# Strassen in a mixture of experts: 512 moving columns per weight tile in the first product, a new layout for the expert phase, a halved last tile

## Chip, cores, metric

One core of one Trainium2 chip. The metric is device time in microseconds (us), median of several executions. Traces are of one execution each. Engines in the profile: PE is TensorE, PEld its weight loads, DVE VectorE, ACT ScalarE, POOL GpSimd, SP the queue of the sync engine. A matmul here has a weight tile of 128 x 128, which is loaded first (98 ns), and 256 or 512 moving columns that pass it; its result goes into a bank (`ps`, 128 x 512 in fp32), from which ACT or DVE takes it (an eviction).

## The reference

Linear attention makes x (4608 tokens x 512), a Sinkhorn routing makes a weight P for each token and expert, and eight experts run densely:

```python
for e in range(E):                       # E = 8, D = 512, F = 1024, N = 4608
    h = np.maximum(x @ w1[e], 0.0)       # first product, "up"
    ye = h @ w2[e]                       # second product, "down"
    out += P[:, e:e + 1] * ye
```

## The kernel before

Tokens go in nine groups of 512. Attention and expert 0 (plain matmuls) share the first 250 us. Experts 1 to 7 use Strassen's scheme with seven products in both up and down. The sums of quadrants that it needs are DVE instructions. The kernel writes its work as a list of operations with their inputs and outputs. A scheduler of its own, which has a model of durations, fixes the order on each engine before the program is built.

```python
    def product(bank, lhs, rhs, nk, r, first, takes=(), wk=()):   # one Strassen product
        for i in range(2):
            for k in range(nk):                    # nk = 2 in up, 4 in down
                pe(256, ... matmul(bank()[:, 256*i:256*i+256], lhsT=lhs(k, i), rhs=rhs(k), ...))

    def up7(A, g, X, hT, r0):                      # one group; fp: pair of feature blocks
        # x1: keep, x2: keep, x3: keep + add, x4: relu all accumulate in the same bank x[fp];
        def keep(fp, n):                           # ACT copies a bank to SBUF
            act(512, ... scalar.copy(out=u[fp][n](), in_=x[fp]()))
        def add(bank, fp, n, i, j):                # DVE: relu(bank + kept copy) -> hT
            dve(515, ... ADD_SAT ...)
        # (cut)
    def down8(e, g, hT, w2):                       # the very last group: plain, four tiles
        for ts in (2, 3, 0, 1):
            py = new("P1")
            # eight matmuls of 512 columns, one eviction (DVE, 512 columns), one store of 256 KB

    ORDER = "X1 x10 w10 x11 X2 x20 y10 x21 Z1 y11 X3 w11 x30 x31 x40 x41 w20 Y1 w21 X4 Z2".split()
    for e in range(1, E):
        # (cut) load_w, sums_w
        for g in (range(NG) if e < E - 1 else [8, *range(8)]):
            X = load_x(g)                          # sums of x, kept in DRAM: four per group
            un = up7(A7, g, X, hT, ["up0"])
            for n in ORDER:                        # up of group g, mixed with down of group g-1
                ...
            dn = down7(e, g, hT, B7)               # seven products, four DVE sums of 1024 elements
```

One pass of ORDER is called a step here: 56 up matmuls and 56 down matmuls of 256 columns.

The softmax here doesn't subtract the row's maximum and nothing guards it: scores larger than these inputs give would overflow.

## Time and profile before

| | before |
|---|---|
| time, median of 6 | 1026.59 us (1026.03 to 1026.82) |
| PE idle in the expert phase | 0.0 us; the matmuls set the pace |
| instructions on PE | 9469 recorded matmuls, 9504 loads |

How to read it: PE is the bound; the prediction shows its lines.

### The profile page before, as it was taken

What the parts mean: (1) busy time and instruction counts of PE and PEld (TensorE: products, weight loads), DVE (VectorE), ACT (ScalarE), POOL (GpSimd) and SP (SyncE); (2) the same over time, 40 slices, a digit from 0 to 9 for tenths busy, and PEclk for the clock granted to TensorE, in tenths of its full rate; (3) what the DMA queues carried; (4) which work ended last, traced back from release to release, by engine and by line L of the source; (5) the groups of instructions that cost most, each with busy time, mean ns of one, the idle gap of its engine ahead of it and who ended that gap; (6) DMA issues with size and microseconds to landing.
All of it is one profiled execution on the core that took longest, in us unless ns stands there. A gap on an engine that the chain in (4) does not pass through costs nothing.

```text
span 1026.8 us, 24281 instructions
## 1 busy us (share of the span) xinstructions
PE 1008.1 (98%) x9469; PEld 837.9 (82%) x9504; DVE 823.5 (80%) x1600; ACT 703.9 (69%) x1530; POOL 458.5 (45%) x480
## 2 busy tenths in 40 slices
PE   7899999999999999999999999999999999999998
PEld 4666666645888888888888888888888888888886
DVE  7999989987888887787777877787778877787775
ACT  7999999834888766666666666666665666666663
POOL 5768664400334444444444434544444433444342
PEclk9999999999999999999999999999999999999999
DMA  9999978170232611161115211341116111614333
GB/s 235 192 197 179 177 137 130 37 154 19 85 104 85 124 42 42 47 129 43 48 46 112 54 43 42 75 102 42 42 46 131 42 42 43 130 36 125 133 124 124
DMA packets 112501, 96.03 MB, mean 94 GB/s; under 512 B 54145, under 2 KB 87041, under 8 KB 112385
## 3 DMA queue, kind: packets, MB, share of 16 engines
q1 hardware_dynamic: 80576, 70.55, 26.5%
q0 software_dynamic: 31648, 23.86, 16.6%
q8 instruction: 74, 1.21, 0.5%
q14 instruction: 43, 0.34, 0.1%
q10 hardware_dynamic: 160, 0.07, 0.0%
HBM read 94.98 MB, written 14.16 MB: 106 GB/s over the span
## 4 chain that ended last, share of the span: by engine, by line
PE 93%; ACT 2%; DVE 1%; DMA 1%; SPq 1%; issue 1%; POOL 0%; DVEq 0%; ACTq 0%
PE ps L1273 74%; PE ps L573 17%; PE ps L856 2%; DMA acc<-in_q_dram 1%; ACT q L569 1%; ACT k L569 0%; SPq L495 0%; ACT wx L569 0%; SPq L551 0%; PE ps L885 0%; DMA xd<-S 0%; DVE ps L864 0%; DVE hT L1305 0%; DVE m L565 0%; POOL wx L761 0%
## 5 line engine op out<-in xcount | busy, mean ns | idle before, releaser
L1428 POOL TENSOR_TENSOR acc<-acc,V 128x512 f32<-128x512 f32 x248 | 314.8, 1280 | 484.5 <-ACT V L1425 426.7
L1301 ACT COPY U<-ps 128x512 f32<-128x512 f32 x378 | 217.0, 586 | 166.2 <-PE ps L1273 150.9
L1305 DVE CUSTOM_DVE_ANT_0 hT<-ps,U 128x512 bf16<-128x512 f32 x378 | 254.6, 687 | 87.7 <-PE ps L1273 59.9
L1425 ACT ACTIVATE V<-ps,P 128x256 f32<-128x256 f32 x496 | 208.1, 473 | 90.7 <-PE ps L1273 82.1
L1413 DVE SCALAR_TENSOR_TENSOR acc<-ps,P,acc 128x256 f32<-128x256 f32 x372 | 159.1, 478 | 69.5 <-PE ps L1273 69.2
L1273 PEld LDWEIGHTS <-S 128*128 128x128 bf16 x1984 | 194.1, 98 | 22.6 <-issue 0.2
L1273 PEld LDWEIGHTS <-T 128*128 128x128 bf16 x1512 | 148.0, 98 | 17.2
L1273 PEld LDWEIGHTS <-hT 128*128 128x128 bf16 x1488 | 145.6, 98 | 16.8
L1273 PE MATMUL ps<-X,T 128*128 128x256 bf16 x1008 | 152.4, 273 | 0.0
L1273 PE MATMUL ps<-T,S 128*128 128x256 bf16 x1056 | 135.8, 273 | 0.0
L1273 PEld LDWEIGHTS <-wx 128*128 128x128 bf16 x1152 | 112.7, 98 | 13.6 <-issue 0.2
L1181 DVE TENSOR_TENSOR S<-hT 128x1024 bf16<-128x1024 bf16 x124 | 87.2, 712 | 10.1 <-ACT hT L1310 9.9
L1273 PEld LDWEIGHTS <-w 128*128 128x128 bf16 x864 | 84.5, 98 | 9.8
L1273 PE MATMUL ps<-xT,wx 128*128 128x256 bf16 x576 | 88.4, 273 | 0.1
L1273 PE MATMUL ps<-X,wx 128*128 128x256 bf16 x576 | 86.8, 273 | 0.0
L1310 ACT ACTIVATE hT<-ps 128x512 bf16<-128x512 f32 x126 | 73.2, 606 | 9.8 <-PE ps L1273 9.8
L1273 PE MATMUL ps<-wx,hT 128*128 128x256 bf16 x560 | 77.6, 273 | 0.0
L1273 PE MATMUL ps<-xT,T 128*128 128x256 bf16 x504 | 76.7, 273 | 0.0
L573 PE MATMUL ps<-xT,w 128*128 128x512 bf16 x270 | 70.5, 379 | 0.7
L573 PE MATMUL ps<-w,hT 128*128 128x512 bf16 x276 | 69.8, 379 | 0.7 <-ACT q L569 0.2
L1273 PE MATMUL ps<-T,hT 128*128 128x256 bf16 x496 | 69.2, 273 | 0.0
L1273 PE MATMUL ps<-xT,w 128*128 128x256 bf16 x432 | 66.5, 273 | 0.0
(129 smaller groups left out, 1426.5 us busy)
## 6 DMA issues: line engine op xcount, KB each, us to landing
X<-xd SPq DMA_DIRECT2D x126, 256.0 KB, 2.7
wx<-in_moe_w_dram POOLq DMA_DIRECT2D x8, 1024.0 KB, 12.4
v_m<-in_v_dram SPq DMA_DIRECT2D x15, 512.0 KB, 5.6
out_dram<-acc SPq DMA_DIRECT2D x14, 512.0 KB, 2.9
w<-in_moe_w_dram POOLq DMA_DIRECT2D x6, 1024.0 KB, 12.1
xd<-S SPq DMA_DIRECT2D x18, 256.0 KB, 2.1
qk<-in_k_dram POOLq DMA_DIRECT2D x12, 256.0 KB, 5.5
qk<-in_q_dram POOLq DMA_DIRECT2D x12, 256.0 KB, 6.4
```

The source lines that it names most:

```text
L569: act(el, lambda: nc.scalar.activation(out=dst(), in_=src(), func=ACT.Exp, bias=0.0, scale=scale), r, w)
L573: nc.tensor.matmul(out_, lhsT=lhsT, rhs=rhs, start=start, stop=stop)
L856: pe(65, lambda j=j: nc.tensor.matmul(pn()[:, j * D1:j * D1 + D1], lhsT=s["T"][x]()[:, j % 2, 2 * h + j // 2, :] if j < 4 else r["T"][x]() ...
L1181: lambda: f.tensor_tensor(out=out_(), in0=x(), in1=y(), op=op), r, w, **kw)
L1273: pe(256, lambda i=i, k=k, z=z: nc.tensor.matmul(bank()[:, 256 * i:256 * i + 256], lhsT=lhs(k, i), rhs=rhs(k), start=first and z, stop=k = ...
L1301: act(512, lambda: nc.scalar.copy(out=u[fp][n]().rearrange("p a b -> p (a b)"), in_=x[fp]()), [x[fp]], [u[fp][n]])
L1305: dve(515, lambda: nc.vector._custom_dve(ADD_SAT, out=out_(fp, i, j), in0=bank[fp]().rearrange("p (a b) -> p a b", a=2), in1=u[fp][n](), s ...
L1310: act(512, lambda: nc.scalar.activation(out=out_(fp, i, j), in_=x[fp]().rearrange("p (a b) -> p a b", a=2), func=ACT.Relu, bias=0.0, scale ...
L1413: dve(320, lambda n=n, ts=ts: nc.vector.scalar_tensor_tensor(out=acc[g][:, ts, 256 * j:256 * j + 256], in0=bank()[:, 256 * n:256 * n + 256 ...
L1425: act(370, lambda n=n: nc.scalar.activation(out=u()[:, n, :], in_=bank()[:, 256 * n:256 * n + 256], func=ACT.Copy, bias=0.0, scale=P[:, 4 ...
L1428: pool(695, lambda: nc.gpsimd.tensor_tensor(out=acc[g][:, 2 * i:2 * i + 2, 256 * j:256 * j + 256], in0=acc[g][:, 2 * i:2 * i + 2, 256 * j: ...
```

## The change

Its intent: fewer, wider matmuls in up (two groups share a weight tile), no X sums loaded for the first expert, buffers fitted to that, and a shorter end. The core of the diff:

```diff
+    hx = hp.tile([128, 8192], BF16, name="hx")          # h of expert 0; later TB, S, V lie over it
+    ring(hp, [128, 4, 512], BF16, "h0", 0, 4, hx, [0])
+    ring(hp, [128, 1024], BF16, "TB", 0, 3, hx, half)
-    ring("s_p", [128, 1024], BF16, "T", 9)
-    ring("s_p", [128, 4, 256], BF16, "S", 5)
+    for slot in range(6):                                # h of the pairs, one tile of six slots
+        ring("s_p", [128, 2, 2, 512], BF16, f"H{slot}", 1)
+    ring("s_p", [128, 1024], BF16, "T", 4)
-    for i in fill:
+    for i in fill[:-8]:                                  # expert 0's last eight down tiles ...
         expert0(i)
+    for i in range(4):
+        up0(8, i)
+    def wide(bank, lhs, rhs, r, first, takes=(), wk=()):
+        for k in range(2):
+            pe(512, lambda k=k: nc.tensor.matmul(
+                bank().rearrange("p (a b) -> p a b", a=2), lhsT=lhs(k), rhs=rhs(k), ...))
     # in down7: four sums of 1024 elements become, for each half fp,
+            sub(dve, 512, s(0), h(1, 0), h(1, 1), ALU.add, ...)
+            sub(dve, 512, h(1, 0), h(0, 0), h(1, 0), ALU.subtract, ...)      # in place
+            sub(dve, 512, s(1), s(0), h(0, 0), ALU.subtract, ...)
+            sub(dve, 512, s(2), h(0, 1), s(1), ALU.subtract, ...)
+        def halves_(ts):                                 # the last tile
+            for part in range(2):
+                tile_(ts, 256 * part, 256)
+                store(g, ts, 1, part)                    # 128 KB, on the ACT queue and on SP
+    END = "X1 p2 Y1 X2 Z1 p3 X3 Z2 X4 p0 p1".split()     # down of group 6 mixed with group 7's tiles
+    early, dn = [plain(8)], plain(7)                     # ... mix with the first Strassen steps
+    pairs = [(g, g + 1) for g in range(0, 8, 2)]
```

Group 8 stays single. All lines of the new kernel are shifted: up's wide matmul is L1316, all matmuls of `product` are L1307, the adds L1364, the copies L1360, the sums L1199.

## The prediction

> **What bounds the kernel now.** I read five views, from coarse to fine. First the page: its busy row, and the chain that ended last.
>
> ```profile
> PE 1008.1 (98%) x9469; PEld 837.9 (82%) x9504; DVE 823.5 (80%) x1600; ACT 703.9 (69%) x1530; POOL 458.5 (45%) x480
> ...
> PE 93%; ACT 2%; DVE 1%; DMA 1%; SPq 1%; issue 1%; POOL 0%; DVEq 0%; ACTq 0%
> ...
> L1273 PE MATMUL ps<-X,T 128*128 128x256 bf16 x1008 | 152.4, 273 | 0.0
> L1273 PE MATMUL ps<-T,S 128*128 128x256 bf16 x1056 | 135.8, 273 | 0.0
> ```
>
> TensorE is busy for all but 18.7 us, and the chain runs through it. The last column of the two groups (idle before) is 0.0: in the Strassen phase no matmul waits. But 98% busy says only that matmuls overlap (273 ns each, far fewer ns apart), so next I took the stages, by windows. Columns: length, then PE, weight load, DVE, ACT, POOL.
>
> ```profile
> 205.85:250.51 44.66, 44.43 (x211) 20.32 (x214) 36.11 (x95) 16.28 (x28) 0.77 (x1) 1.00 0.41 89
> 250.51:258.68 8.17, 8.10 (x73) 7.03 (x72) 5.25 (x11) 7.45 (x14) 0.00 (x0) 1.00 0.29 98
> 258.68:1015.20 756.52, 756.52 (x6929) 677.87 (x6929) 590.99 (x1062) 489.65 (x1024) 324.06 (x260) 1.00 0.30 74
> 1015.20:1026.80 11.60, 7.02 (x33) 3.02 (x31) 4.08 (x7) 0.00 (x0) 0.58 (x1) 0.93 0.48 182
> ```
>
> From 258.68 to 1015.20 TensorE is never idle at full clock; DVE is at 78% and ACT at 65%. The idle time before 205 us is in attention, which the change does not touch. What is left to win: the rhythm of the matmuls, about 0.5 us around the start of the phase, and the tail. Third, the rhythm, from the chain in order of time and the timeline:
>
> ```profile
> 258.68 756.68 PE ps L1273 x6928
> ```
>
> ```profile
> 219.31 1.89 PE L573 MATMUL ps<-xT,w 128*128 128x512 bf16 x8
> 221.03 1.89 PE L573 MATMUL ps<-w,hT 128*128 128x512 bf16 x8
> ...
> 241.66 8.51 PEld L573 LDWEIGHTS <-hT 128*128 128x128 bf16 x40
> ...
> 241.88 8.79 PE L573 MATMUL ps<-w,hT 128*128 128x512 bf16 x39
> ...
> 250.51 0.60 PE L1273 MATMUL ps<-xT,wx 128*128 128x256 bf16 x4
> ```
>
> A matmul of 256 columns costs 756.52 / 6928 = 109.2 ns. One of 512 costs (250.51 - 241.88) / 40 = 215.75 ns (40 loads; one matmul record is missing). The eight between 219.31 and 221.03 give 215 ns. I use 215.7. Two of 256 are 218.4, so a merge of two saves 2.7 ns. Lastly the tail, timeline:
>
> ```profile
> 1015.20 7.07 PE L573 MATMUL ps<-wx,hT 128*128 128x512 bf16 x31
> ...
> 1018.33 5.09 SPq L1151 DMA_DIRECT2D out_dram<-acc  x4
> ...
> 1022.31 0.75 DVE L1362 SCALAR_TENSOR_TENSOR acc<-ps,P,acc 128x512 f32<-128x512 f32 x1 [0.91 <-PE ps L573]
> ```
>
> The last matmul ends at 1022.27, its eviction at 1023.06, the span at 1026.8: 4.5 us of eviction, store and end.
>
> [...]Here loads take 98 ns under a matmul of 109 ns and never hold one up; the rhythm decides[...]. [...]In the trace, 1024-element differences start 0.60 us apart and 512-element ones 0.33. [...]The trace has 2.6 us median from issue to landing for a 256 KB store, with its data moved in some 0.7 us.
>
> **The change, part by part.**
>
> *Wide products.* The code's first product (up) is seven Strassen products of 8 matmuls, 56 per group and expert; the second (down) is 56 too. Check: 63 up steps and 62 down steps give 7000 matmuls, the sum of the counts of that line on the page. Of nine groups, eight are paired: 7 experts x 8 groups x 56 = 3136 matmuls of 256 columns become 1568 of 512. Saving: 1568 x 2.7 ns = 4.2 us, all on the path, since TensorE alone sets the time there. The 1568 loads that fall away (98 ns each) were hidden and give nothing. The ninth group and all downs stay at 256. A pair of steps does the same arithmetic: one step goes from 112 x 109.2 = 12.23 us to 28 x 215.7 + 56 x 109.2 = 12.16 us.
>
> *Evictions.* The same count and size: per step six copies on ACT, six adds on DVE, two relus. A PSUM bank now holds two groups of one feature block instead of two feature blocks of one group.
>
> *Down's sums on DVE.* Four of 1024 elements become eight of 512: 8 x 0.33 - 4 x 0.60 = +0.24 us per step of 12.16. By starts, DVE has now about 6 x 0.60 adds + 6 x 0.41 reads + 4 x 0.60 sums + 0.53 weight sums = 9.0 us of 12.2; then 9.2, or 76%. By busy records it goes from 78% to some 82%. Off the path.
>
> *Memory.* Each expert loads three X tiles per pair rather than four; the first loads none, using them where they were made. SP loads drop from 126 x 256 KB to an estimated 81 x 256 KB. Those loads land in 2.7 us behind 12 us steps, so nothing. T shrinks from nine buffers to four: three are in use by one expert, one is spare, so the next expert's second and third weight sums must wait for products in the old expert's last step. The code asks for s2 and s3 before the next first product. Their buffers come free about mid-step, some 5 us early; a sum takes 0.6. I expect no stall.
>
> *The phase's start.* Expert 0's last eight down tiles (8 x 1.73 = 13.8 us) may now mix with the first Strassen steps. Before, those steps had no down work, and 250.51 to 258.68 has 72 matmuls, worth 7.86 us: 0.3 us lost. Routing ends at 242.6, four weight sums at about 245, so the tiles also fill what comes before. Gain 0.2 us.
>
> *The tail.* Work on TensorE is the same (8 x 215.7 against 16 x 109.2 for the last tile, +0.02). The last eviction falls from 0.75 to an estimated 0.44 (the trace's 256-column one), and 128 KB moves in about half of 0.7 us. That is 0.65 us. But group 6's 1 MB of output used to leave from 1015.5, under seven us of matmuls; now its down ends just ahead of the last two tiles, so that 1 MB and the tiles share the DMA engines at 400 GB/s in the last 4 us, which may return half. Gain 0.3 us.
>
> Sum: 4.2 + 0.2 + 0.3 = 4.7 us. I set 0.3 us against it for new short waits where the fixed order no longer fits: 1026.47 - 4.4 = 1022.1.
>
> **The rivals.** (1) *Evictions become the bound.* Two matmuls fill a bank in 0.43 us, one more DVE instruction per two; the order was made from a model of times. For: DVE at 80%, its share of the chain 1%, waits of ACT behind DVE of 14.8 us in the phase. Against: fill time per bank is the same, and TensorE waited 0.0 us before. A wait of 0.1 us in each of 62 steps gives back everything and makes 1028; a wait of 0.05 makes 1025. (2) *Buffers.* A stall at each of six changes of expert, from T or the single-buffered S tiles, at 0.5 to 1 us: 1025 to 1028. For: no spare memory. Against: the time in hand worked out above. (3) *The gain is hidden anyway*: if a strided moving operand (two runs of 256) costs a few ns at the seam, the wide matmul takes 218 and the time is 1026. No row of this trace shows such an operand, neither for nor against. (4) *More than the rhythm*: if loads took time that 109.2 ns hides, halving them would give 1568 x 98 = 154 us, or -15%.[...]
>
> **Range and chances.** The floor is everything working: 4.2 + 0.3 + 0.65 = 5.2 us, 1021.3, less scatter. Runs of before differ by 0.8 us. Upward lie the waits of rivals 1 and 2, which I think partial and unlikely. Range 1020.6 to 1025.0. 2% is 20.5 us; only a breakdown of the order, or rival 4, gets there: faster 0.02, within 0.96, slower 0.02.
>
> **What would show it.** Wide matmuls 215 to 216 ns apart (218 or more proves rival 3); some 5432 matmuls in the phase; TensorE idle still near 0.0 us between experts (else rival 2) and within steps (rival 1); DVE's busy share near 82%; the phase about 4 us shorter; the last eviction 0.44 us, and under 4.5 us from last matmul to end. If the time is below 1020 or above 1026, an amount or a wait that I have not seen is at work.

4.2 + 0.2 + 0.3 = 4.7 us, less 0.3 for waits, 4.4, and 1026.47 - 4.4 = 1022.1. Each term was worked out or estimated from the trace of before. There the DMA engines move 399 to 412 GB/s at their peaks between 990 and 1027 us, and the last 256 KB store moves its data between 1023.9 and 1024.7 us.

## More of the kernel before

DVE is the nearest other engine. Its groups, from the page (instruction, count, busy us, mean ns of one, idle before it and who ended that):

```profile
L1305 DVE CUSTOM_DVE_ANT_0 hT<-ps,U 128x512 bf16<-128x512 f32 x378 | 254.6, 687 | 87.7 <-PE ps L1273 59.9
...
L1181 DVE TENSOR_TENSOR S<-hT 128x1024 bf16<-128x1024 bf16 x124 | 87.2, 712 | 10.1 <-ACT hT L1310 9.9
```

The adds wait for PE, not PE for them. The sums take 685 ns as a rule; the mean of 712 hides a few long ones (up to 947 ns), which come up again under fill_first.

## The result, and the profile after

| | before | after |
|---|---|---|
| time, median of 6 | 1026.59 us | 1022.57 us (1021.99 to 1022.86) |
| ratio | | 0.9961, 95% interval 0.9948 to 0.9974 |

Ratios are the mean time of one kernel's runs over that of the other's of the same rounds, so not quite the ratio of the medians. The class is "same" (within 2%), and the interval lies below 1.

The page of the changed kernel: busy row, chain, and groups.

```profile
PE 1007.1 (99%) x7944; PEld 686.1 (67%) x7944; DVE 853.2 (84%) x1833; ACT 701.6 (69%) x1530; POOL 466.8 (46%) x480
...
PE 95%; ACT 2%; DVE 1%; issue 0%; POOL 0%; DMA 0%; DVEq 0%; ACTq 0%
...
L1364 DVE CUSTOM_DVE_ANT_0 hs<-ps,U 128x512 bf16<-128x512 f32 x378 | 253.0, 687 | 35.7 <-PE ps L1316 15.0
...
L1316 PE MATMUL ps<-X,T 128*128 128x512 bf16 x448 | 129.0, 379 | 0.3 <-ACT U L1360 0.2
...
L1199 DVE TENSOR_TENSOR hx<-hx,hs 128x512 bf16<-128x512 bf16 x124 | 64.2, 518 | 0.0
```

PE has 1560 fewer loads than before and the same bound. DVE rose from 80 to 84% of the span. The idle time ahead of its adds fell from 87.7 to 35.7 us: it still keeps up, with less in hand. By windows (length; PE, PEld, DVE, ACT, POOL busy):

```profile
203.95:258.15 54.20, 54.20 (x264) 24.56 (x261) 41.90 (x101) 27.01 (x48) 0.98 (x2) 1.00 0.32 64
258.15:1013.95 755.80, 755.47 (x5410) 529.02 (x5407) 622.19 (x1302) 484.14 (x1017) 332.36 (x260) 1.00 0.24 59
1013.95:1020.70 6.75, 3.21 (x24) 2.06 (x21) 2.59 (x5) 0.00 (x0) 0.34 (x1) 0.95 0.61 233
```

PE idles 0.33 us in 755.8, DVE is at 82%. To compare the two traces, I cut both at the same work. The 32 matmuls of the last gate end attention; the timeline has them at

```profile
204.83 0.94 PE L573 MATMUL ps<-wgate,xT 128*128 128x8 bf16 x32
```

before, and after at

```profile
203.15 0.95 PE L581 MATMUL ps<-wgate,xT 128*128 128x8 bf16 x32
```

| stretch, us | before | after | difference |
|---|---|---|---|
| start to last gate | 204.83 | 203.15 | -1.68 |
| last gate to end of last matmul ("phase") | 817.44 | 814.01 | -3.43 |
| end of last matmul to end of span ("tail") | 4.50 | 3.58 | -0.92 |

The first row is taken as scatter: nothing there changed, and over the eleven other profiled executions, whose attention work is that of one of these two kernels, it came out anywhere from 202.65 to 204.48. Before's 204.83 lies just above all of them; its profile fell into a run of 1028.55 us, 2 us above its median. So the change made 3.43 + 0.92 = 4.35 us by the trace, against 4.0 by the medians.

The tail of after, in the timeline:

```profile
1013.95 3.21 PE L581 MATMUL ps<-wx,hs 128*128 128x512 bf16 x22
...
1015.51 1.29 DVE L1424 SCALAR_TENSOR_TENSOR acc<-ps,P,acc 128x512 f32<-128x512 f32 x2 [0.49 <-PE ps L581]
...
1016.84 0.35 ACTq L1163 DMA_DIRECT2D out_dram<-acc  x1
1017.19 0.48 DVE L1424 SCALAR_TENSOR_TENSOR acc<-ps,P,acc 128x256 f32<-128x256 f32 x1 [0.39 <-PE ps L581]
1017.71 0.33 SPq L1163 DMA_DIRECT2D out_dram<-acc  x1
```

The last eviction is 0.48 us and no longer 0.75, and the last store lands 2.00 us after its issue and no longer 2.53.

Within the phase I read the distances between starts of neighbouring matmuls, as means over all that have no gap. A 256-column one takes 109.16 ns in both kernels, the wide one 215.84 ns. Gaps are what exceeds the usual distance of a shape by over 15 ns (places where a matmul record is missing are left out): 0.54 us in all before, 1.01 us after. This finds more than the PE idle time above, since a matmul's record lasts 273 or 379 ns and covers short gaps. Most of the latter lie here:

```profile
261.88 1.03 PE L1316 MATMUL ps<-xT,wx 128*128 128x512 bf16 x4
...
262.51 0.59 ACT L1360 COPY U<-ps 128x512 f32<-128x512 f32 x1 [0.86 <-PE ps L1316]
...
263.14 0.38 PE L1316 MATMUL ps<-X,T 128*128 128x512 bf16 x1 [0.24 <-ACT U L1360]
```

The next product goes into the same bank and waits for the copy out of it (0.40 us). One gap of 0.23 us, at 837.7, is not explained: nothing that the profile shows was waited for there. So the account of the phase is: 1568 x (2 x 109.16 - 215.84) = 1568 x 2.48 = 3.89 us won, 0.47 lost to gaps, 0.02 to the last tile's eight more matmuls: 3.40, against 3.43 measured.

### The profile page after: what moved, and what is told of

It reads as the page before. It is cut to its first block, busy times and chain, and to the rows that moved or that the text cites. A ratio compares the mean times of both kernels' runs of the same rounds, so it can differ in the third digit from the quotient of the medians.

```text
span 1020.7 us, 21372 instructions
## 1 busy us (share of the span) xinstructions
PE 1007.1 (99%) x7944; PEld 686.1 (67%) x7944; DVE 853.2 (84%) x1833; ACT 701.6 (69%) x1530; POOL 466.8 (46%) x480
## 4 chain that ended last, share of the span: by engine, by line
PE 95%; ACT 2%; DVE 1%; issue 0%; POOL 0%; DMA 0%; DVEq 0%; ACTq 0%
PE ps L1307 41%; PE ps L1316 33%; PE ps L581 18%; PE ps L864 2%; PE ps L711 0%; ACT q L577 0%; DVE m L573 0%; ACT k L577 0%; DVE wx L573 0%; DMA acc<-in_k_dram 0%; PE ps L893 0%; ACT kr L577 0%; ACT wx L577 0%; DVE xb L878 0%; PE ps L903 0%
## 5 line engine op out<-in xcount | busy, mean ns | idle before, releaser
L1516 POOL TENSOR_TENSOR acc<-acc,hx 128x512 f32<-128x512 f32 x248 | 322.9, 1309 | 476.7 <-ACT hx L1513 473.3
L1360 ACT COPY U<-ps 128x512 f32<-128x512 f32 x378 | 216.6, 588 | 134.1 <-PE ps L1316 117.6
L1513 ACT ACTIVATE hx<-ps,P 128x256 f32<-128x256 f32 x496 | 208.0, 476 | 124.6 <-PE ps L1307 112.0
L1364 DVE CUSTOM_DVE_ANT_0 hs<-ps,U 128x512 bf16<-128x512 f32 x378 | 253.0, 687 | 35.7 <-PE ps L1316 15.0
L1307 PEld LDWEIGHTS <-hs 128*128 128x128 bf16 x1984 | 194.1, 98 | 72.8 <-issue 0.2
L1307 PEld LDWEIGHTS <-hx 128*128 128x128 bf16 x1488 | 145.6, 98 | 40.0 <-issue 0.2
L1307 PE MATMUL ps<-hx,hs 128*128 128x256 bf16 x992 | 132.5, 273 | 0.0
L1316 PE MATMUL ps<-X,T 128*128 128x512 bf16 x448 | 129.0, 379 | 0.3 <-ACT U L1360 0.2
L1316 PE MATMUL ps<-xT,wx 128*128 128x512 bf16 x384 | 101.5, 379 | 0.0
L1316 PEld LDWEIGHTS <-T 128*128 128x128 bf16 x672 | 65.8, 98 | 48.0 <-issue 0.3
L1307 PE MATMUL ps<-wx,hs 128*128 128x256 bf16 x560 | 80.4, 273 | 0.0
L1316 PEld LDWEIGHTS <-wx 128*128 128x128 bf16 x512 | 50.1, 98 | 38.4 <-issue 0.5
L1316 PE MATMUL ps<-xT,w 128*128 128x512 bf16 x288 | 75.6, 379 | 0.0
L1307 PE MATMUL ps<-wx,hx 128*128 128x256 bf16 x496 | 68.4, 273 | 0.0
L1316 PE MATMUL ps<-xT,T 128*128 128x512 bf16 x224 | 66.0, 379 | 0.0
L1307 PE MATMUL ps<-hx 128*128 128x256 bf16 x496 | 64.3, 273 | 0.1
L1199 DVE TENSOR_TENSOR hx<-hx,hs 128x512 bf16<-128x512 bf16 x124 | 64.2, 518 | 0.0
L1307 PE MATMUL ps<-w,hs 128*128 128x256 bf16 x432 | 62.7, 273 | 0.0
```

The lines of the kernel that those rows point to most:

```text
L1199: lambda: f.tensor_tensor(out=out_(), in0=x(), in1=y(), op=op), r, w, **kw)
L1307: pe(256, lambda i=i, k=k, z=z: nc.tensor.matmul(bank()[:, 256 * i:256 * i + 256], lhsT=lhs(k, i), rhs=rhs(k), start=first and z, stop=k = ...
L1316: pe(512, lambda k=k: nc.tensor.matmul(bank().rearrange("p (a b) -> p a b", a=2), lhsT=lhs(k), rhs=rhs(k), start=first and k == 0, stop=k ...
L1360: act(512, lambda: nc.scalar.copy(out=u[q][n]().rearrange("p a b -> p (a b)"), in_=x[q]()), [x[q]], [u[q][n]])
L1364: dve(515, lambda: nc.vector._custom_dve(ADD_SAT, out=out_(q, i, j), in0=bank[q]().rearrange("p (a b) -> p a b", a=2), in1=u[q][n](), s0=3 ...
L1513: act(370, lambda n=n: nc.scalar.activation(out=u()[:, n, :], in_=bank()[:, 256 * n:256 * n + 256], func=ACT.Copy, bias=0.0, scale=P[:, 4 ...
```

## The experiments

Eleven kernels ran. The diffs are shortened; "..." marks what is left out. Times are medians with the ratio to before of the same rounds; "phase", "tail" and "gaps" as above.

**split.** The wide matmul as two of 256, the rest as changed.

```diff
-        for k in range(2):
-            pe(512, ... matmul(bank() as (a b), lhsT=lhs(k), rhs=rhs(k), ...))
+        for k in range(2):
+            for a in range(2):
+                pe(256, ... matmul(bank()[:, 256 * a:256 * a + 256], lhsT=lhs(k), rhs=rhs(k)[:, a], ...))
```

> The changed kernel, with each wide matmul of 512 columns issued as two of 256 with the same weights, into the two halves of the same bank; memory, order of the work and tail stay. Rhythm theory: 3136 matmuls at 109.16 ns in place of 1568 at 215.84 ns, so +3.9 us, about 1026.4 us; the sum of the idle gaps of TensorE stays under 1.5 us. Rival, that the new layout and the fewer X loads gave the gain: about +0, 1022.6 us. Rival, that the weight loads cost time of their own: well over +4 us.

Measured: 1027.61 us, ratio 1.0003 (0.9989 to 1.0016). Phase 817.68, tail 3.66, gaps 0.76.

```profile
PE 1010.5 (99%) x9512; PEld 838.9 (82%) x9512; DVE 856.9 (84%) x1833; ACT 700.6 (68%) x1530; POOL 463.8 (45%) x480
```

The phase is 3.67 us longer than after, or 3.9 with its 0.25 us fewer gaps counted back. That is the rhythm and nothing else. The time is 1.2 us above the expected 1026.4; in the profiled run 1.3 us of that are attention (last gate at 204.48, after's at 203.15), which this edit does not touch. The 1568 loads more (153 us of PEld) cost no more than this. Layout, X loads and order without wide matmuls leave the phase at 817.68 against 817.44 before: they win nothing there.

**seam.** The moving operand as one run of 512 columns (wrong result).

```diff
-                     lambda k: rhs()[:, :, k, :], ...)           # two runs of 256
+                     lambda k: flat(y, k), ...)                  # one run of 512 of the same tile
```

> The changed kernel with the moving operand and the bank of each wide matmul as one run of 512 columns in place of two runs of 256; the result is wrong on purpose. Wide matmuls start 215.84 ns apart in the changed kernel, the plain ones of expert 0 215.75. If the seam costs the difference: 215.75 ns here, 0.1 us in all. If the seam is what takes the saving per merge from the predicted 2.7 ns to the measured 2.5: 215.6 ns.

Measured, one look (state unknown, 1022.28 us, relative error 1.19 as intended): the distance is 215.83 ns, phase 814.02. The seam of two runs costs nothing here (215.84 ns with it), and neither expectation came true: the 0.1 ns over expert 0's plain matmuls is not the seam. What it is stays open; it is 0.15 us in all.

**tail_alone.** Before, with the halved last tile only.

```diff
-        for ts in (2, 3, 0, 1):          # four tiles of 512, one store each
+        for ts in (2, 3, 0):
+            tile_(ts, 0, 512); store(g, ts, 1)
+        for part in range(2):
+            tile_(1, 256 * part, 256); store(g, 1, 1, part)
```

> The kernel before with nothing but the halved last tile and its two stores on two queues. If the halving is worth 0.9 us by itself: 1025.7 us, and 3.6 us from last matmul to end. If it needs the new order of the end (or if the stores of group 6 were in its way): within 0.3 us of before.

Measured: 1026.11 us, ratio 0.9993 (0.9981 to 1.0006). Phase 817.46, tail 3.64. The rounds can't show 0.9 us; the trace can: 0.86 us off the tail with the old order of the end.

**whole_last.** After, with the last tile whole.

```diff
-                "p1": lambda: halves_(1)}
+                "p1": lambda: whole(1)}
```

> The changed kernel with its last tile whole again: one of 512 columns, one eviction, one store of 256 KB. If the halving alone makes the shorter tail (3.58 us from the end of the last matmul to the end of the span, 4.50 before): +0.9 us, 1023.5 us, with an eviction of 0.75 us and 2.5 us to landing. If the order of the end makes it: +0.3 us or less.

Measured: 1023.14 us, ratio 0.9965 (0.9953 to 0.9978). Phase 813.99, tail 4.24. Its last eviction and store:

```profile
1015.97 1.99 SPq L1169 DMA_DIRECT2D out_dram<-acc  x2
1016.85 0.75 DVE L1424 SCALAR_TENSOR_TENSOR acc<-ps,P,acc 128x512 f32<-128x512 f32 x1 [0.91 <-PE ps L581]
```

The tail grows by 0.66 us, less than the 0.9 expected: 0.27 by the eviction, 0.34 by the landing (2.34 us, not 2.5), 0.05 at the end. So the halving makes most of the 0.92; the last 256 KB store of before landed 0.2 us later than this one (2.53 us, and 2.51 in before_sums_twice, which has the same end), for a reason I did not find.

**quarters.** After, with the second half of the last tile cut into two of 128 columns.

```diff
-                tile_(ts, 256 * part, 256); store(g, ts, 1, part)          # part 0, 1
+            tile_(ts, 0, 256);   store(g, ts, 1, 0)
+            tile_(ts, 256, 128); store(g, ts, 1, 1)
+            tile_(ts, 384, 128); store(g, ts, 1, 2)
```

> The changed kernel with the last half tile (256 columns) cut again into two of 128. If the tail is eviction plus bytes: last matmul to end of span falls from 3.58 to some 3.35 us (eviction 0.48 to 0.35, a store of 64 KB in place of 128), and eight more matmuls cost 0.02 us; the time falls by 0.2 us, which the rounds can't show. If the store is all fixed time: no change of its 2.0 us to landing.

Measured: 1023.38 us, ratio 0.9969 (0.9954 to 0.9984). Tail 3.65: the eviction fell to 0.35 us as expected, but the 64 KB store took 2.27 us to land, not less than 2.0. Cutting further brought nothing. It doesn't show that a small store is slower: four stores were still in flight when this one was issued, against three in the changed kernel, of which one landed 0.1 us later.

**fill_first.** After, with expert 0's last eight down tiles before the Strassen steps, as in the old kernel.

```diff
-    for i in fill[:-8]:
+    for i in fill:
         expert0(i)
-    for i in range(4):
-        up0(8, i)
     # plain(7), plain(8): nothing left to do in the first two steps
```

> The changed kernel with expert 0's last eight down tiles put back ahead of the Strassen steps. The prediction took their mixing for a gain of 0.2 us; the trace of the changed kernel instead has gaps of 0.40 and 0.19 us at the end of the mixed stretch. If mixing helps: +0.2 us, 1022.8 us, with gaps over 0.3 us where steps without down work begin. If mixing made the gaps: -0.4 us, 1022.2 us, and under 0.3 us of gaps between 204 and 280 us.

Measured: 1024.42 us, ratio 0.9977 (0.9965 to 0.999). Phase 816.02, gaps 3.03. I had two expectations and both were small; the mixing is worth 2.0 us. Two places in its timeline carry it:

```profile
259.97 1.08 PE L1314 MATMUL ps<-X,T 128*128 128x512 bf16 x4
...
260.60 0.69 DVE L1197 TENSOR_TENSOR X<-xT 128x1024 bf16<-128x1024 bf16 x1
260.88 1.11 ACT L1358 COPY U<-ps 128x512 f32<-128x512 f32 x2
261.55 0.59 PE L1314 MATMUL ps<-X,T 128*128 128x512 bf16 x2 [0.50 <-ACT U L1358]
...
274.69 1.27 POOL L1514 TENSOR_TENSOR acc<-acc,hx 128x512 f32<-128x512 f32 x1 [0.39 <-ACT hx L1511]
274.75 1.49 DVE L1197 TENSOR_TENSOR hs<-hs 128x512 bf16<-128x512 bf16 x1
...
277.08 1.24 PE L1314 MATMUL ps<-xT,wx 128*128 128x512 bf16 x5 [0.80 <-DVE acc L1499]
```

First, in a step without down work, PE had nothing to do while a bank was copied out (0.50 us before 261.55, until ACT's copy had ended). Pairs make two such steps in a row, before there was one. Second, a 512-element difference on DVE took 1.49 us in place of 0.42. It began while a GpSimd instruction ran (274.69, 1.27 us) and ended 0.28 us after that one; the evictions behind it came late, and PE waited 0.80 us for one. The other traces show the like: in the changed kernel 22 of the 500 differences of 512 elements are over 80 ns longer than usual. All 22 began while a GpSimd instruction ran, and ended a median of 0.28 us after it. Of 25 others that began during one, 23 did so in its last 0.1 us; two began within 0.13 us of its start and were not held up, which I can't explain. The long sums of before are of this kind too: 15 of 304, all begun during a GpSimd instruction and ended a median of 0.55 us after it. What holds them up, the runs do not show.

**fill_first_noscale.** The same without the ACT instructions that scale the accumulators of groups 0 to 7 (wrong result).

```diff
-        if e == 1 and g < 9:
+        if e == 1 and g < 9 and g >= 8:
             for ts in range(4):
                 act(670, ... acc[g][:, ts, :] *= P[:, 4 * g + ts, 0:1])
```

> The fill_first kernel without the four ScalarE instructions per group that scale the accumulators of groups 0 to 7 (wrong result on purpose). In fill_first 1.7 us of gaps on TensorE lie between 259 and 264 us, in the second of two steps without down work. ScalarE had some 7.0 us of work in such a step of 6.0 us of matmuls, 4.3 us without the scaling. If ScalarE makes the gaps: under 0.4 us of them there, and 1.5 us less time than fill_first. If the adds and sums on DVE make them: they stay above 1 us.

Measured: 1023.35 us, ratio 0.9966 (0.9949 to 0.9982). Phase 814.76, gaps 1.75. In the place in question, by windows, fill_first had

```profile
259.00:265.00 6.00, 5.06 (x21) 1.92 (x20) 4.97 (x10) 5.18 (x10) 0.00 (x0) 1.00 0.24 90
```

and this one has

```profile
259.00:265.00 6.00, 5.45 (x28) 2.46 (x27) 5.58 (x11) 3.71 (x7) 0.00 (x0) 1.00 0.23 87
```

ACT has less to do (5.18 to 3.71 us), but of 1.7 us of gaps 1.1 stay, by the second clause of the expectation. So ACT's scaling is a part. With it gone, DVE is busy for 5.58 of 6.00 us, and PE still waits for copies. How the rest divides between DVE and the chain through one bank was not separated. The 0.96 us gap at 275.9 is gone as well. That the long DVE instruction is a matter of how DVE and GpSimd happen to meet is my reading; it was not tested by itself.

**sums_twice, sums_4more, sums_2more.** After, with six, four or two more of the same 512-element sums per step (each writes the value that it wrote already).

```diff
             sub(dve, 512, s(2), h(0, 1), s(1), ALU.subtract, ...)
+            sub(dve, 512, s(2), h(0, 1), s(1), ALU.subtract, ...)     # 2more: this; 4more: s(1) too; twice: s(0) too
```

> The changed kernel with six of the eight 512-element sums of each down step computed twice (same values): six more DVE instructions per step, 2.0 us more of DVE by starts in a step of 12.16 us (9.2 becomes 11.2). If DVE has the slack that the prediction saw (off the path): under +2 us of time and under 2.5 us of gaps on TensorE after the gates. If evictions on DVE were about to bind (rival 1): more than +10 us, with gaps on TensorE in every step.

> The same with two of the four sums twice: four more DVE instructions, 1.3 us by starts (10.5 of 12.16 us). Between the two others: by a straight line from no cost at +0.24 us to 44 us at +2.0 us, some +20 us; if the cost sets in late, under +5 us.

> The changed kernel with one of its four sums computed twice for each half: two more DVE instructions per step, 0.66 us by starts (9.2 becomes 9.9 of 12.16 us). If the margin of DVE begins to run out only near the whole 2.0 us that cost 44 us: under +1.5 us against the changed kernel and gaps on TensorE after the gates under 2 us. If the changed kernel already sits at the edge: +10 us or more.

| | more on DVE per step, by starts | time, us | ratio to before | phase against after, us |
|---|---|---|---|---|
| sums_2more | 0.66 | 1026.26 | 0.9997 (0.9982 to 1.0012) | +3.5 |
| sums_4more | 1.3 | 1039.79 | 1.0125 (1.0109 to 1.0142) | +16.2 |
| sums_twice | 2.0 | 1067.16 | 1.0392 (1.0377 to 1.0408) | +43.1 |

My expectation of slack fell. What PE waited for, in sums_twice (us in total, times, longest):

```profile
PE ps L1307 <- ACT hx L1519: 8.8, 17, 1.0
PE ps L1307 <- DVE hx L1199: 4.9, 8, 0.9
...
PE ps L1307 <- DVE hs L1364: 3.8, 6, 1.5
PE ps L1316 <- ACT U L1360: 2.8, 7, 0.7
PE ps L1316 <- DVE hs L1364: 2.8, 3, 1.6
```

They are evictions and sums, on two engines. In sums_2more most of the cost lies between 263 and 325 us, in the first expert, where DVE also makes the X sums. sums_2more and sums_4more fell between the clauses of their expectations. The expectation of sums_4more also has a wrong sum: its line from 0.24 to 2.0 us gives 26 us at 1.3, not 20. A line from nothing to 43.1 us at 2.0 would give 14 us at 0.66 and 28 us at 1.3, where 3.5 and 16.2 were measured: the cost sets in below 0.66 us and grows faster than in proportion.

**before_sums_twice.** The kernel before, with three of its four 1024-element sums twice.

```diff
         sub(dve, 1024, lambda: S[3](), a(0, 1), lambda: S[1](), ALU.subtract, ...)
+        sub(dve, 1024, lambda: S[3](), a(0, 1), lambda: S[1](), ALU.subtract, ...)     # S[1], S[2] too
```

> The kernel before with three of its four 1024-element sums per step computed twice: 1.8 us more of DVE by starts (9.0 becomes 10.8 of 12.23 us). If the change used up slack that the kernel before had (fewer buffers, more DVE instructions): well under +20 us against before. If the slack was as small before: +30 to +45 us.

Measured: 1098.08 us, ratio 1.0696 (1.0679 to 1.0713). Phase 71.3 us longer than before, more than either clause of the expectation. With 1.8 us more of DVE, PE waited for

```profile
PE ps L1273 <- DVE hT L1305: 26.1, 13, 4.7
PE ps L1273 <- DVE acc L1419: 14.1, 6, 2.7
PE ps L1273 <- ACT V L1431: 6.1, 7, 1.0
```

The granted clock fell to 0.986: the trace has half clock in seven stretches of 3.4 to 6.8 us, in which 106 matmuls start 213 ns apart in place of 109. That is about 11 of the 71 us; waits make the rest. The changed kernel, with 2.0 us more and full clock, loses 43.1. So the change did not use up slack at this load: it bears extra DVE work better. A small load, as in sums_2more, was not tried on before. That fits sums in halves, which can start before the second half of h is there, and a down step that lags further behind its up. Neither was tested by itself.

## Why the prediction was right

The time (1022.57 against 1022.1, range 1020.6 to 1025.0) is inside, and the mechanism is the one named. The sum held partly because terms erred in opposite ways.

- **Wide products, 4.2 us.** Right in kind, 8% high: measured 3.89, shown by split. I took 109.20 ns from a stretch divided by its count, which contained 0.2 us of gaps, and 215.7 from plain matmuls; the distances are 109.16 and 215.84. On 1568 merges, tenths of a nanosecond count.
- **Loads that fall away give nothing.** Right: split puts 1568 of them back and pays for the rhythm only. Rival 4 is out, and rival 3 (a costly seam) by seam.
- **The phase's start, +0.2 us.** Wrong in sign. Gaps there and later grew by 0.47 us; with the 0.3 us that the prediction set aside for short waits, its net was 0.1 us lost. The tiles that I saw as a small bonus are a repair: without them (fill_first) the new layout has 2.5 us more gaps than before, and mixing wins 2.0 of them back. I had not seen that pairs bring two steps without down work.
- **The tail, 0.3 us.** Too low: 0.92. My gross figure of 0.65 is what whole_last shows (0.66). I took half away for contention with group 6's megabyte, which did not happen: its last store landed at 1017.82 us, when the last store had just been issued (1017.71), and that landed in 2.00 us. The fear was not empty: in sums_4more and sums_twice group 6's last store landed 1.4 and 2.2 us after the issue of the very last one, which then took 2.32 and 2.74 us. The eviction took 0.48 us, as 256-column ones did before (468 to 486 ns); the prediction's 0.44 was misread.
- **Buffers.** Right: no gap between experts beyond 0.08 us. One expert takes 109.48 us in the chain of after, the sum of eight pair steps and a single one (8 x 12.155 + 12.23 = 109.47):

```profile
492.96 2.16 PE ps L1316 x10
...
602.44 2.16 PE ps L1316 x10
```

- **DVE off the path.** Right for this change (82% in the phase as predicted, PE idle for 0.33 us there), but my ground for it, 9.2 us of 12.16 by starts, suggested 3 us in hand. The series of sums shows that 0.66 us more costs 3.5 us. Rival 1 was nearer than I wrote.

What stays open: 0.35 us between the trace's 4.35 and the medians' 4.0, which is within the scatter of attention; the 0.1 ns between wide and plain matmuls; the gap at 837.7; the landing of before's last store.

## What to carry to other kernels

Where matmuls stood back to back, as here, widening them won only what two narrow ones took beyond one wide one: 2.5 ns for each one saved (2 x 109.16 - 215.84). Count the merges before laying out memory anew. A busy share of 80% on an evicting engine that runs a fixed order was not 20% of slack (DVE at 82% in the phase: 0.66 us more in a step of 12.16 cost 3.5 us): add a known load to it and see where the time starts to rise. And when work is grouped in larger units, look at the steps that lose their companion work, for the gaps moved there (1.7 us of fill_first's 3.03 between 259 and 264 us).
